# Memory rows in two parts, another order of block 1's tail units, and a cap on filling work

## The chip, the core and the metric

The kernel runs on one core of a Trainium2 chip. Its engines work side by side, each through its own instructions in order: TensorE (PE in the profile, PEld for its weight loads), VectorE (DVE), ScalarE (ACT), GpSimd (POOL) and SyncE (SP), which here only issues DMAs. They wait for each other through semaphores. Matmuls write PSUM; DVE and ACT read it. The metric is the device time of one execution in microseconds (us), as the median of some runs. The profile is of one execution.

## The reference

A sequence of 2048 rows of width 640 goes through an attention with a recurrent memory, in segments of 32 rows, and then through a feed-forward part. In short (layer norms and residual sums around it):

```python
for s in range(64):
    h = concat([mem, x[32*s:32*s+32]])         # 8 memory rows + 32 rows
    q, k, v = h @ Wq, h @ Wk, h @ Wv           # 32 heads of 128
    scores = q @ k.T * scale                   # masked: memory sees all,
    p = softmax(where(mask, scores, -1e9))     # rows see memory and their past
    o = (p @ v) @ Wo                           # 40 x 640
    mem = o[:8]                                # needed by the next segment
    outs.append(o[8:])
h = x + concat(outs)
out = h + relu(layernorm(h) @ w1 + b1)**2 @ w2 + b2
```

The memory rows make the 64 segments a chain: segment s+1 can't project its memory rows before segment s has its output.

## The kernel before

**Steps and blocks.** A step is a segment; four steps are a block of 128 rows. Of a segment, `step` (L445) handles the 8 memory rows and the first 24 rows together as 32 rows of `hT`. The last 8 rows, the tail, are projected for a whole block at once (32 rows): `tail_units` (L316) for their q, k and v, and `wo_tail_units` (L355) for their output. Tail work doesn't belong to the chain of memory rows. It is cut into units of four to eight matmuls, kept in the list `fill`, and PE gets some of them wherever a step would leave it waiting.

**A step, on PE, in order.** Projections for q, k, q, k (two halves each, L466), 20 matmuls each; memory scores of the first half (`sm`); values `v`; scores of the second half; token scores; one or two filling units; memory values (`values`, L516); two units; 64 matmuls of the output projection of the memory rows and of the segment before (`pw`, L652); two units; token values of the step before (`token_values`, L408); all units left; then the next step's q projection into the tile `pq`.

**From pw to the next hT.** `wo_out` (L271) sums the four row groups of `pw`: ACT copies the upper two to `otmp` (L281), then the lower two (L282), DVE adds `pw` and `otmp` into `o` (L283). `mem_to_hT` (L370) turns `o` into the columns of `hT` (L374). All four work on 160 columns, which are five column chunks (DC = 5) of 32. The q projection takes its chunks one after the other: matmuls of chunk c need only chunk c of `hT`. `pw`, `pq` and `sm` are tiles of the pool `chn` with one buffer, so each of them waits until the one before has been read.

**What sets the order.** The code's order is the order on each engine. `portion(s)` (L872) takes units from `plan`, which is sorted by due step, at a pace of 8 a step; a unit that is due is taken in any case. It can take more than 8 where the pace had fallen behind. `late` holds small works for DVE (turns of tail rows among them) that run at the start of a step.

**The start.** `start` (L775) projects segment 0 while the weights come in, and between them the tail values of blocks 0 to 11, then q and k of block 1's tails, as far as PE has time; what is left goes to `fill` for step 0, which (`ready`) runs ten units ahead of its values and `SEG0[k]` units ahead of each quarter of its `pw`. The quarters need the eight pieces of `wo` in the order of their loads (L149). Tail values are cast from PSUM by ACT to a tile and written to DRAM (`vt_d`, L337), from where they are read again later. Eighteen places of tiles that are not in use yet are `parked` for this (blocks 1 to 9, two each). Without a parked place the row goes into one of four buffers of `row` (L247), which also take every q and k row on its way from PSUM (ACT, L244 and L251) to DVE's turn (L256). All these DMAs are issued by SP in the order of the code; at most eight are under way, as each waits for the landing of the eighth before it.

Of the kernel before, what the change touches and what calls it, by code (L numbers as in the profile page):

```python
# [9 lines left out]
ALU = mybir.AluOpType  # L10
# [6 lines left out]
def kernel(  # L17
# [16 lines left out]
    nc = tc.nc  # L34
# [3 lines left out]
    SEG = 32  # L38
# [4 lines left out]
    DC = D // 128  # L43
# [95 lines left out]
    for q in range(4):  # L139
        nc.vector.tensor_copy(out=o0[32 * q:32 * q + 32, :].rearrange("m (c f) -> m c f", f=32),  # L140
                              in_=mem0[:].rearrange("m (c q f) -> m q c f", q=4, f=32)[:, q])
# [80 lines left out]
    def proj(w, by, lhs, n, ps, c0, c1):  # L222

        if by == "columns":
            wr = w[:].rearrange("p (c g j n k e) -> p c n k g j e", c=DC, g=G, n=2, j=4, k=4)
        elif by == "half":
            wr = w[:].rearrange("p (c k j n e) -> p c n k j e", c=DC, k=G, n=2, j=4)
        else:
            wr = w[:].rearrange("p (c k n f) -> p c n k f", c=DC, k=G, n=2)
        for c in range(c0, c1):  # L230
            for k in range(4):
                nc.tensor.matmul(ps[32 * k:32 * k + 32, :], lhsT=lhs(c), rhs=wr[:, c, n, k], start=(c == 0), stop=(c == DC - 1))  # L232

    def mmtile():
        return mm.tile([128, 512], F32, tag="mm", name="ps")
# [32 lines left out]
                    nc.tensor.matmul(pw[32 * j:32 * j + 32, c0:c0 + DH], lhsT=lhs(p), rhs=wov2[:, head(p), ch],  # L268
                                     start=(h == 0), stop=(h == 15))

    def wo_out(pw):  # L271
        o = o_ring[0]
        o_ring.append(o_ring.pop(0))
        tmp = s2.tile([128, DQ], F32, tag="otmp", name="otmp")

        def blocks(p0, p1, c0):
            return pw[p0:p1, c0:c0 + DH].rearrange("p (c x) -> p c x", x=64)[:, :, 0:32]

        def five(x):
            return x.rearrange("p (c f) -> p c f", f=32)  # L280
        nc.scalar.copy(out=five(tmp[0:64]), in_=blocks(64, 128, 0))  # L281
        nc.scalar.copy(out=five(tmp[64:128]), in_=blocks(0, 64, 64))  # L282
        nc.vector.tensor_tensor(out=five(o[:]), in0=blocks(0, 128, 32), in1=five(tmp[:]), op=ALU.add)  # L283
        return o

    fill, late, mid, nook = [], [], [], []
# [1 line left out]
    def run(q, n, held=None, stop=False):  # L288
        while n > 0 and q:
            out = q.pop(0)()  # L290
            if out and held is not None:
                held.append(out)
                if stop:
                    break
            elif out:
                out[1]()
            n -= 1
# [15 lines left out]
    def tail_rows(b, c):  # L313
        return hTts[b // 4][:, c, b % 4].rearrange("p k s -> p (k s)")

    def tail_units(b, which):  # L316
        w = {"q": wq, "k": wk, "v": wv}[which]
        lhs = lambda c: tail_rows(b, c)
        st = {}

        def unit(n, c):
            def f():
                if c == 0:
                    st[n] = mmtile()
                proj(w, "columns" if which != "v" else "order", lhs, n, st[n], c, c + 1)
                return (True, lambda: tail_out(b, which, n, st[n][:])) if c == DC - 1 else None
            return f
        return [unit(n, c) for n in range(2) for c in range(DC)]
# [38 lines left out]
            return f  # L367
        return [unit(k) for k in range(10)]

    def mem_to_hT(o, b, sp):  # L370

        at = sp * SEG
        hc = hTs[b % 2][:].rearrange("p (c r) -> p c r", c=DC)
        nc.vector.transpose(out=hc[:, :, at:at + SEG], in_=o[:].rearrange("p (c f) -> p c f", f=32))  # L374

    def tails_in(b, sp, n=None):
        hs = slice(0, H) if n is None else slice(n * 16, n * 16 + 16)
# [67 lines left out]
    def step(b, sp, v=None):  # L445
        s = b * 4 + sp
# [3 lines left out]
        if not ready:  # L450
            v = s2.tile([128, EG], BF16, tag="v", name="v")
# [178 lines left out]
        if nook:  # L630
# [9 lines left out]
                                op=ALU.mult)  # L640
        pk = s1.tile([128, HG, 32], BF16, tag="pk", name="pk")
        nc.gpsimd.tensor_tensor(out=pk[:], in0=ek[:, :, 0:SEG], in1=rk[:].unsqueeze(2).to_broadcast([128, HG, SEG]),
                                op=ALU.mult)

        if not last:
            pw = chn.tile([128, 512], F32, tag="ch", name="pw")
            if ready:
                for k in range(4):
                    run(fill, SEG0[k])
                    wo_rounds(lambda p: oT[:, p, M:NK], pw, [2 * k + h + 4 * (k // 2) for h in (0, 1, 4, 5)])  # L650
            else:
                wo_rounds(lambda p: oT[:, p, M:NK], pw, range(16))  # L652
            o = wo_out(pw)
            mem_to_hT(o, (s + 1) // 4, (s + 1) % 4)
            if s > 1:
                store_main(o, s - 2)
            held = []
            run(fill, 2, held)
            if s:
                token_values(s - 1, *prevs[-2], po, False)  # L660
                token_out(s - 1, po)
            run(fill, 100, held)
            settle(held, True)
            for _, f in held:
                late.append((0.35, f, s + 1))
            tails_in((s + 1) // 4, (s + 1) % 4)
# [5 lines left out]
        for u in range(2):  # L672
            nc.gpsimd.tensor_tensor(out=pTx[:, u], in0=pTt[:, u, 0:TL].unsqueeze(1).to_broadcast([128, 4, TL]),
                                    in1=same[:], op=ALU.mult)
# [48 lines left out]
    parked += [(hnT0[:, c, :], True) for c in range(DC)] + [(ht0[k][:, 0:512], True) for k in range(NK4)]  # L723
    parked += [(t, True) for t, _ in halves(oTts[1][:].rearrange("p h r -> p (h r)"))]
    writes = []
    SEG0 = (0, 0, 8, 8)
    hnTs = [hnT0[:], ck(DC * NT).rearrange("p (c t) -> p c t", c=DC)]
    ots = [ck(D) for _ in range(4)]
    fxs = [ck(D) for _ in range(4)]
# [45 lines left out]
    def start():  # L775

        v = s2.tile([128, EG], BF16, tag="v", name="v")
        main = rows_of(0, 0)
        pas = [pop.tile([128, 2, 512], F32, tag="po%d" % h, name="pa%d" % h) for h in range(2)]
        banks = [pas[h][:, n, :] for h in range(2) for n in range(2)]  # L780
        banks += [mmtile()[:] for _ in range(3)] + [chn.tile([128, 512], F32, tag="ch", name="pv")[:]]
        for c in range(DC):
            for k in range(4):
                for n in range(2):
                    proj(wv, "order" if k else "half", (lambda c, b=k - 1: tail_rows(b, c)) if k else main, n,
                         banks[2 * k + n], c, c + 1)
        for n in range(2):
            evac(n == 1, v[:, n * 512:(n + 1) * 512], banks[n])
        for k in range(1, 4):
            for n in range(2):  # L790
                tail_out(k - 1, "v", n, banks[2 * k + n], n == 1)
        units = tail_units(3, "v")
        run(units, DC)
        ln_transpose(("t", 1))()
        ln_norm(("t", 2))
        run(units, DC)
        units += [u for b in range(4, 8) for u in tail_units(b, "v")]

        def stream(which, w, dst, turn=None):
            pas = [pop.tile([128, 2, 512], F32, tag="po%d" % h, name="pa%d" % h) for h in range(2)]  # L800
            for c in range(DC):
                for n in range(2):
                    proj(w, "columns", main, n, pas[0][:, n, :], c, c + 1)
                for n in range(2):
                    proj(w, "columns", lambda c: tail_rows(0, c), n, pas[1][:, n, :], c, c + 1)
                if c == 2 and turn:
                    turn()
                if c < DC - 1:
                    run(units, 7 + c % 2)
            run_late(0, 100)  # L810
            for n in range(2):
                row = rowtile()[:]
                evac_row(which, row, pas[0][:, n, :])
                tail_out(0, which, n, pas[1][:, n, :])
                flip(row, dst, n)
                run_late(0, 100)
                if which == "k":
                    tails_in(0, 0, n)

        stream("q", wq, qT, lambda: ln_transpose(("t", 2))())  # L820
        for n in range(2):
            spread(n)
        tails_v_in(0, nc.gpsimd, 0, 1)
        run(units, 10)
        parked.append((s1.tile([128, D], BF16, tag="xn", name="parkx")[:, 0:512], False))
        units += [u for b in range(8, 12) for u in tail_units(b, "v")]
        stream("k", wk, kT)
        units += tail_units(1, "q") + tail_units(1, "k")
        run(units, 10)
        fill.extend(units)  # L830
        return v
# [28 lines left out]
    for b in range(2, NB):  # L860
        for which in "qk":
            u = tail_units(b, which)
            plan += [(4 * b - 3 + (which == "k"), 4 * b - 5, u[DC * n:DC * n + DC]) for n in range(2)]
    for b in range(12, NB):
        u = tail_units(b, "v")
# [6 lines left out]
    def portion(s):  # L872
        n = round(8.0 * (s - 2)) - paced[0]
        got = []
        while True:
            if not begun:
                ready = [p for p in plan if p[1] <= s]
                if not ready:
                    break
                plan.remove(ready[0])  # L880
                begun.append(ready[0])
            d, _, u = begun[0]
            if len(got) >= n and d > s:
                break
            got.append(u.pop(0))
            if not u:
                begun.pop()
        paced[0] += len(got)
        return got
# [57 lines left out]
    for t in range(S // NT):  # L947
        hnT = hnTs[t % 2]
        more = t + 1 < S // NT
        got, hts, mvs = {}, {}, {}  # L950
        if t == 0:
            got = got1
# [3 lines left out]
        for fc in range(FC):  # L956
# [13 lines left out]
            if more and fc >= 1 and (fc - 1) // 3 < NK4:  # L970
                k, stage = divmod(fc - 1, 3)
# [30 lines left out]
        for q in range(NK4):  # L1002
            pr, hf = q // 2, q % 2
            cs = slice(hf * DH, (hf + 1) * DH)
# [4 lines left out]
            for hh in range(2):  # L1009
                k = pr + 2 * hh  # L1010
# [44 lines left out]
```

## Time and profile before

| | us |
|---|---|
| median of three runs | 981.39 (980.9 to 983.57) |
| the profiled execution: its time | 980.93 |
| its span, first to last instruction | 979.1 |
| PE busy | 939.5 |
| DVE, ACT, POOL busy | 652.7, 525.1, 282.1 |
| mean granted PE clock | 0.995 |

How it is read: in the groups, the waits and the timeline a line names an engine, a line of the kernel, an operation and the tiles that it writes and reads. In the waits, the numbers are us in total, how many times, and the longest. In the timeline, the first two numbers are the start and the length in us, and brackets hold the idle time before and what ended it. Steps 1 to 63 lie between 73 and 847 us, about 12.2 us each; the feed-forward part fills the end.

### The profile page before, as it was taken

How to read it: one execution, taken by the hardware profiler on the slowest of the kernel's cores; microseconds unless marked ns; L12 is line 12 of the kernel's file. 1: busy time of each engine (PE TensorE's matmuls, PEld its weight loads, DVE VectorE, ACT ScalarE, POOL GpSimd, SP SyncE). 2: the span in 40 equal slices, each digit the busy share in tenths (PEclk: the TensorE clock that was granted, in tenths of full speed). 3: DMA queues.
4: the chain of work that ended last, by engine and by line, in shares of the span. 5: the costliest groups of instructions: out<-in, count | busy, mean ns of one | idle time of the engine just before them, and what ended most of it. 6: DMA issues, size and time to landing. Idle time of an engine off the chain costs nothing.

```text
span 979.1 us, 55574 instructions
## 1 busy us (share of the span) xinstructions
PE 939.5 (96%) x24760; PEld 547.4 (56%) x24760; DVE 652.7 (67%) x1942; ACT 525.1 (54%) x1271; POOL 282.1 (29%) x870
## 2 busy tenths in 40 slices
PE   6948999999999999999999999999999999999998
PEld 2425555555555555555555655555555656555555
DVE  5137777777676767776767676777776787566542
ACT  2425555566556556566656565665655655523321
POOL 2112323233223232323232323232323233263210
PEclk9979999999999999999999999999999999999999
DMA  9980110101010201010101010101010211543320
GB/s 355 400 273 28 14 31 9 30 15 31 14 37 14 31 13 31 9 31 8 31 14 31 14 31 11 33 12 33 11 33 6 53 40 24 165 137 79 98 55 27
DMA packets 65871, 56.62 MB, mean 58 GB/s; under 512 B 37384, under 2 KB 61712, under 8 KB 63712
## 3 DMA queue, kind: packets, MB, share of 16 engines
q1 hardware_dynamic: 65392, 52.74, 19.3%
q8 instruction: 194, 3.18, 1.4%
q14 instruction: 45, 0.37, 0.1%
q0 software_dynamic: 224, 0.33, 0.1%
q10 hardware_dynamic: 16, 0.01, 0.0%
HBM read 38.37 MB, written 9.44 MB: 49 GB/s over the span
## 4 chain that ended last, share of the span: by engine, by line
PE 84%; DVE 6%; DMA 4%; ACT 3%; SPq 2%; issue 1%; POOL 0%; ACTq 0%; DVEq 0%
PE ps L232 26%; PE pw L268 16%; PE px L232 12%; PE pq L232 7%; PE y L1012 6%; PE ps L960 6%; PE ps L268 3%; PE po L522 2%; DMA wq<-in_A_Wq_dram 2%; PE po L415 2%; SPq L149 2%; DVE kT L476 1%; PE sm L486 1%; DMA wo<-in_A_Wo_dram 1%; PE ps L575 1%
## 5 line engine op out<-in xcount | busy, mean ns | idle before, releaser
L232 PEld LDWEIGHTS <-hT 128*32 128x32 bf16 x7680 | 193.7, 96 | 189.9 <-DVE hT L374 23.2
L268 PE MATMUL pw<-wo,oT 128*32 128x320 bf16 x4224 | 161.9, 301 | 13.1 <-DVE oT L242 11.2
L232 PE MATMUL ps<-wk,hT 128*32 128x512 bf16 x2520 | 157.8, 379 | 0.0
L268 PEld LDWEIGHTS <-oT 128*32 128x32 bf16 x4224 | 118.9, 97 | 53.1 <-DVE oT L242 28.8
L256 DVE STREAM_TRANSPOSE qT<-row 128x512 bf16<-128x512 bf16 x128 | 90.7, 709 | 58.4 <-ACT row L251 55.0
L639 POOL TENSOR_TENSOR pkt<-ek,rk 128x64 bf16<-128x64 bf16 x64 | 18.9, 296 | 284.1 <-DVE rk L637 284.1
L232 PE MATMUL ps<-wv,hT 128*32 128x512 bf16 x1260 | 89.7, 378 | 0.0
L232 PE MATMUL pq<-wq,hT 128*32 128x512 bf16 x1260 | 79.5, 381 | 8.6 <-DVE hT L374 6.3
L244 ACT CAST row<-ps 128x512 bf16<-128x512 f32 x105 | 61.7, 590 | 37.8 <-PE ps L232 37.3
L426 ACT CAST oT<-po 128x512 bf16<-128x512 f32 x128 | 68.7, 589 | 20.4 <-PE po L420 18.9
L232 PE MATMUL px<-wq,hT 128*32 128x512 bf16 x1260 | 79.0, 379 | 0.0
L232 PE MATMUL px<-wv,hT 128*32 128x512 bf16 x1260 | 79.0, 378 | 0.0
L434 POOL COPY qz<-qT 128x96 bf16<-128x96 bf16 x126 | 33.6, 267 | 154.8 <-DVE qT L256 154.8
L968 ACT ACTIVATE wv<-ps,b1f 128x512 bf16<-128x512 f32 (+1 forms) x56 | 37.6, 672 | 66.6 <-PE ps L960 65.3
L633 ACT ACTIVATE ek<-tk 128x320 bf16<-128x320 f32 x64 | 30.1, 471 | 74.9 <-DVE tk L628 66.5
L256 DVE STREAM_TRANSPOSE kT<-row 128x512 bf16<-128x512 bf16 x65 | 46.2, 711 | 32.2 <-ACT row L244 32.0
L232 PEld LDWEIGHTS <-hTt 128*32 128x32 bf16 x1920 | 46.2, 96 | 27.9 <-issue 2.3
L1012 PE MATMUL y<-wq,wk 128*128 128x320 bf16 x416 | 58.9, 299 | 0.2
L473 ACT CAST row<-ps 128x256 bf16<-128x256 f32 x126 | 40.8, 375 | 28.5 <-PE ps L232 28.5
L251 ACT ACTIVATE row<-px 128x512 bf16<-128x512 f32 x63 | 37.6, 597 | 30.2 <-PE px L232 30.2
L486 PEld LDWEIGHTS <-qz 128*32 128x32 bf16 x2016 | 34.8, 94 | 32.4 <-POOL qz L436 3.7
L251 ACT ACTIVATE row<-pq 128x512 bf16<-128x512 f32 x63 | 37.6, 597 | 25.5 <-PE pq L232 25.0
(129 smaller groups left out, 1674.7 us busy)
## 6 DMA issues: line engine op xcount, KB each, us to landing
wv<-in_A_Wv_dram SPq DMA_DIRECT2D x5, 1024.0 KB
wq<-in_A_Wq_dram SPq DMA_DIRECT2D x5, 1024.0 KB
wk<-in_A_Wk_dram SPq DMA_DIRECT2D x5, 1024.0 KB
wo<-in_A_Wo_dram SPq DMA_DIRECT2D x8, 640.0 KB
o_all<-o SPq DMA_DIRECT2D x256, 7.5 KB
vt<-vt_d SPq DMA_DIRECT2D x60, 64.0 KB
xt<-in_A_x_dram SPq DMA_DIRECT2D x19, 160.0 KB
wq<-in_B_w_dram SPq DMA_DIRECT2D x1, 2080.0 KB
```

Of the source, the lines that this page charges most:

```text
L232: nc.tensor.matmul(ps[32 * k:32 * k + 32, :], lhsT=lhs(c), rhs=wr[:, c, n, k], start=(c == 0), stop=(c == DC - 1))
L244: nc.scalar.copy(out=out_, in_=in_)
L251: nc.scalar.mul(out=row, in_=ps, mul=scale)
L256: nc.vector.transpose(out=dst[:, n * 16:(n + 1) * 16, 0:32], in_=row.rearrange("p (h e) -> p h e", e=32))
L268: nc.tensor.matmul(pw[32 * j:32 * j + 32, c0:c0 + DH], lhsT=lhs(p), rhs=wov2[:, head(p), ch], start=(h == 0), stop=(h == 15))
L426: nc.scalar.copy(out=oTg[:, gs, :, 0:SEG], in_=po[1][h][:, :, 0:256].rearrange("p g (i q) -> p g i q", q=32))
L434: nc.gpsimd.tensor_copy(out=d.rearrange("p a (j f) -> p a j f", j=3)[:, :, :, 0:M], in_=src[:, :, 0:3, :])
L473: nc.scalar.copy(out=row[:, u * 256:(u + 1) * 256], in_=ps[:, u * 256:(u + 1) * 256])
L486: nc.tensor.matmul(sm[32 * g:32 * g + 32, 0:NK], lhsT=qz[:, p, :], rhs=kT[:, p, :], start=(j == 0), stop=(j == 3), skip_group_check=True)
L960: nc.tensor.matmul(ps[:], lhsT=w1[:, c, fc * 128:(fc + 1) * 128], rhs=hnT[:, c, :], start=(c == 0), stop=(c == DC - 1))
L968: nc.scalar.activation(out=r[:, 0:w], in_=ps[:, 0:w], func=ACT.Relu, bias=b1f[:, fc:fc + 1], scale=1.0)
L1012: nc.tensor.matmul(y[hh][:, 0:DH], lhsT=f1T[:, fc, k * 128:(k + 1) * 128], rhs=w2[:, fc, cs], start=(fc == 0 and not hf), stop=(fc == FFUL ...
```

## The change

Three parts.

1. `wo_out` gets a second argument, `then`. With it, the two copies, the add and the turn into `hT` are done for column chunks 0 to 2 (96 columns) and then for chunks 3 and 4 (64 columns). `step` uses that for the memory rows; the tails' output (`wo_tail_out`) and the last step's `end_output` still use one part.
2. In `start`, the tail values of blocks 8 and 9 and block 1's tail queries come ahead of `stream("k", ...)`, then block 1's tail keys, then the tail values of blocks 10 and 11. `SEG0`, which gives the units ahead of the quarters of step 0's `pw`, is (0, 1, 8, 9) where it was (0, 0, 8, 8); as it is a maximum, all that is left is run.
3. A portion is closed at nine units, unless the next one is due.

```diff
-    def wo_out(pw):
+    def wo_out(pw, then=None):
...
-        nc.scalar.copy(out=five(tmp[0:64]), in_=blocks(64, 128, 0))
-        nc.scalar.copy(out=five(tmp[64:128]), in_=blocks(0, 64, 64))
-        nc.vector.tensor_tensor(out=five(o[:]), in0=blocks(0, 128, 32), in1=five(tmp[:]), op=ALU.add)
+        for c0, c1 in ((0, 3), (3, DC)) if then else ((0, DC),):
+            cs = slice(c0, c1)
+            nc.scalar.copy(out=five(tmp[0:64])[:, cs], in_=blocks(64, 128, 0)[:, cs])
+            nc.scalar.copy(out=five(tmp[64:128])[:, cs], in_=blocks(0, 64, 64)[:, cs])
+            nc.vector.tensor_tensor(out=five(o[:])[:, cs], in0=blocks(0, 128, 32)[:, cs], in1=five(tmp[:])[:, cs], op=ALU.add)
+            if then:
+                mem_to_hT(o, *then, cs)
         return o
...
-    def mem_to_hT(o, b, sp):
+    def mem_to_hT(o, b, sp, cs=slice(0, DC)):
...
-        nc.vector.transpose(out=hc[:, :, at:at + SEG], in_=o[:].rearrange("p (c f) -> p c f", f=32))
+        nc.vector.transpose(out=hc[:, cs, at:at + SEG], in_=o[:].rearrange("p (c f) -> p c f", f=32)[:, cs])
...
-            o = wo_out(pw)
-            mem_to_hT(o, (s + 1) // 4, (s + 1) % 4)
+            o = wo_out(pw, ((s + 1) // 4, (s + 1) % 4))
...
-    SEG0 = (0, 0, 8, 8)
+    SEG0 = (0, 1, 8, 9)
...
-        units += [u for b in range(8, 12) for u in tail_units(b, "v")]
+        units += [u for b in (8, 9) for u in tail_units(b, "v")] + tail_units(1, "q")
         stream("k", wk, kT)
-        units += tail_units(1, "q") + tail_units(1, "k")
+        units += tail_units(1, "k") + [u for b in (10, 11) for u in tail_units(b, "v")]
...
-            if len(got) >= n and d > s:
+            if len(got) >= min(n, 9) and d > s:
```

## The prediction

> **What bounds the kernel now.** I read the page's chain of waits first, then the waits, then the timeline in three places. PE carries nearly the whole chain, so only time in which PE stands still can be won, and what makes it stand longer is lost.
>
> ```profile
> PE 939.5 (96%) x24760; PEld 547.4 (56%) x24760; DVE 652.7 (67%) x1942; ACT 525.1 (54%) x1271; POOL 282.1 (29%) x870
> PE 84%; DVE 6%; DMA 4%; ACT 3%; SPq 2%; issue 1%; POOL 0%; ACTq 0%; DVEq 0%
> ```
>
> The waits name what the change touches: a long stop in step 0 and a short one at each step's end.
>
> ```profile
> PEld L268 <- DVE oT L242: 28.8, 59, 10.1
> ...
> PEld L232 <- DVE hT L374: 23.2, 55, 1.9
> ...
> ACT row L251 <- DMA vt_d<-row: 9.9, 1, 9.9
> ```
>
> **The stop in step 0**, in the chain's pieces in order of time, and in the timeline:
>
> ```profile
> 50.14 10.31 DMA wo<-in_A_Wo_dram
> ...
> 60.51 2.84 DMA vt_d<-row
> ...
> 63.43 0.60 ACT row L251
> ```
>
> ```profile
> 65.60 2.32 PE L268 MATMUL pw<-wo,oT 128*32 128x320 bf16 x32 [9.96 <-DVE oT L242]
> ...
> 73.09 1.26 PE L232 MATMUL pq<-wq,hT 128*32 128x512 bf16 x20 [1.54 <-DVE hT L374]
> ```
>
> PE is said to wait for DVE; the root is a buffer. The four `row` buffers hold the tail values of blocks 10 and 11, whose writes stand in SP's queue behind the `wo` loads. Block 1's tail queries need such a buffer, and ACT, in order, can't copy oT before the write lands at 63.35. The clock falls meanwhile, as busy times by stage show (a line ends with granted clock, DMA share, GB/s):
>
> ```profile
> 54.90:58.30 3.40, 0.74 (x48) 0.35 (x40) 0.00 (x0) 0.00 (x0) 0.00 (x0) 1.00 1.07 359
> 58.30:65.60 7.30, 0.00 (x1) 0.01 (x2) 1.54 (x4) 1.24 (x3) 0.00 (x0) 0.50 0.99 296
> 65.60:68.60 3.00, 3.00 (x44) 1.58 (x48) 1.96 (x5) 0.47 (x1) 0.25 (x1) 0.51 0.41 102
> ```
>
> **A step's end**, steps 27 to 28:
>
> ```profile
> 405.62 0.29 ACT L281 COPY otmp<-pw 64x160 f32<-64x160 f32 x1 [0.62 <-PE pw L268]
> ...
> 405.92 0.28 ACT L282 COPY otmp<-pw 64x160 f32<-64x160 f32 x1
> ...
> 406.24 0.33 DVE L283 TENSOR_TENSOR o<-pw,otmp 128x160 bf16<-128x160 f32 x1 [0.48 <-ACT otmp L282]
> ...
> 406.60 0.35 DVE L374 STREAM_TRANSPOSE hT<-o 128x160 bf16<-128x160 bf16 x1
> ...
> 407.00 1.26 PE L232 MATMUL pq<-wq,hT 128*32 128x512 bf16 x20
> ```
>
> The last pw matmul starts 0.34 before the first copy, so from it to pq are 1.72 us. PE's own work in between takes, by the boundaries that it limits, 1.92 us with 6 filling units, 2.35 with 8, 2.79 with 10: 0.66 + 0.212 per unit, thus 1.72 with the usual 5. The fill just covers the chain of copies. Seven boundaries with at most two units stand open; there PE starts pq 0.93 to 1.27 us after its matmul before:
>
> ```profile
> 97.27 1.05 PE L232 MATMUL pq<-wq,hT 128*32 128x512 bf16 x16 [1.03 <-DVE hT L374]
> ```
>
> **The change part by part.** The sum is against the profiled execution, 980.93 us (span 979.1 and 1.83 around it); it lies 0.46 under the median, 981.39.
>
> *Two parts at the step's end.* Each of 63 steps gets two ACT and two DVE instructions more. Two things in the changed program's waits decide. pq and pw share the one `ch` buffer, so pq's first weight load waits for the last reader of pw, which is now the second add, not the first turn. And ACT's third copy waits for the first add on DVE, as both touch the same `otmp`. So six instructions lie in a row: copy, copy, add (96 columns), copy, copy, add (64 columns); both turns fall off the path (the second is done 0.3 us after pq starts and wanted 0.6 after). Durations of 96 and 64 columns are not in the trace. For the copies I take the line through ACT's PSUM rows (128 columns 266 ns, 256 375, 512 589: 0.84 a column), set at the 289 and 284 of 160: 235 and 230, then 208 and 203. For the adds the line from 324 at 160 to 423 at 256 (L625), 1.03 a column: 257 and 224. Between two copies lie 12 ns, ACT to DVE 32, DVE to ACT 35 (L492 to L495 where ACT has no wait ahead of it), DVE to pq 58. From the last pw matmul: 342 + 235 + 12 + 230 + 32 + 257 + 35 + 208 + 12 + 203 + 32 + 224 + 58 = 1880 ns, against 1720: 0.16 later. In the changed order 53 of the 62 boundaries after steps 1 to 62 have five units or fewer: 53 x 0.16 = 8.5 us; three with a little more (0.06 to 0.11 each) 0.2; six with six units are covered by PE's 1.93. Sum +8.6, the shift of units among boundaries included. Ends: every copy at ACT's shortest row (203, one element) and every add at 181 (L492, 40 columns) gives 1.70, -0.7 us; copies along the line from 203 at one element to 287 at 160 give 1.99, +15 us. The value stands nearest to rows of the same kind. Behind ACT's waiting third copy stand the fourth, the two oT casts (L426), a filling row and pq's row: the casts start 0.2 us later (1.58 after the last pw matmul, was 1.37), and px, which needs their PSUM, starts 1.2 us after they end; pq's row isn't ready sooner than ACT. DVE's pTt and pTk come 0.4 later and are wanted a step on. That costs nothing; without this cover it would be 0.2 a step, 13 us.
>
> [...]
>
> *Block 1's tail queries ahead of the last tail values, SEG0 (0, 1, 8, 9).* The number of units, rows, turns and writes stays; their places change. The queries' and keys' rows now find free buffers, so nothing holds ACT in step 0. The ten units before the values still end by 55.2; DVE has two key turns (0.7 each) before its oT cast, 54.4 + 1.4 + 0.3 = 56.1, and pw starts there, not at 65.60. Its 64 matmuls (4 x 0.5) and ten units (2.1) would end at 60.2, but the last `wo` piece lands at 60.45: last pw matmul 60.95, pq 62.8. Then the stall comes back: the value rows of blocks 10 and 11 are written in step 0, into the buffers that step 1's q and k rows need. Their four writes are moved behind nine issues of SP: four parked writes, the x load and four vt loads, at the intervals these had before (62.52 to 68.07): 60.51 + 4 x 0.51 + 0.53 + 4 x 0.70 = issue at 65.9. After vt loads a write landed 2.35 us after its issue (68.07 to 70.40): 68.25. Behind the waiting q row on ACT stand the rows of k and of the second halves, each on a write of its own, 0.5 apart; DVE's turns, POOL's spread and PE's scores wait for them. ACT copies q (0.6), DVE turns q (0.7), then k (0.7): scores at 70.4. Before, pq at 73.09 gave scores at 77.42. PE's own pace from 62.8 would be 67.1, so it stands 3.3 us. Won: 7.0, less 0.25 as the second half's rows come late: -6.7. Ends: landing after 1.95 to 2.84 us, -7.1 to -6.2. The clock: it fell at 58.3, 2.7 us after PE stopped, and half speed held to 68.6; a 3.1 to 3.3 us stand can do the same for up to 3.4 us, 0 to 1.7 lost; I take +0.9.
>
> [...]
>
> *Portions capped at 9.* PE's total work is unchanged; units move among steps 7 to 20 and 61, 62. None of the open boundaries gets a unit. What it gives: two units ahead of the values instead of one (steps 13, 17 to 20) save some 0.15 to 0.23 each, as the second values then follow the first after 0.015 instead of 0.16 to 0.24; step 62 gets a first unit (0.33), step 14 gains 0.05. Sum -1.35; ends -0.7 and -1.6.
>
> Sum: 980.93 + 8.6 - 6.7 + 0.9 - 1.35 = 982.4, for the median 0.46 more: 982.8.
>
> **The rivals.**
> 1. *Slower: small instructions hardly get cheaper.* Place: the six at each boundary. At 1.99 us the loss is 15: 989.2. It decides from 1.91, where 10.1 is lost. For it: ACT's one-element row takes 203. Against: its casts fall steadily down to 128 columns.
> 2. *The row wait in step 1 isn't there* (the writes land in time). Then 10.25 is won and no clock lost: 978.4. For: the DMA share falls to 0.41 from 65.6 on. Against: SP's order and the 2 us of every landing.
> 3. *The chain is shorter than before:* copies overlap. [...] The pairs of casts at L426 and L473 do overlap by 0.10; taken off both pairs here, 1.67, no loss but 0.5 won: 973.7. Against: in all 82 pairs L281, L282 the second starts 12 ns after the first ends.
>
> **How the numbers follow.** Forecast 0.62, own range 980 to 986 (0.45 of it within 0.3%, 0.17 above); rival 1 0.20; rival 2 0.08 (half of it faster, half within); rival 3 0.10, most of it faster. Hence faster 0.13, same 0.50, slower 0.37, where 0.3% (2.9 us) is about what a measurement of this kernel can tell from no change. The range leaves out rival 3 and the top of rival 1: 978 to 988.
>
> **What would show it.** Right: the first otmp copy to pq 1.54 us instead of 1.38 at boundaries with five units; four copies of about 0.2; the ACT wait for vt_d<-row moved from 63.4 to about 68, some 4 us long, on pq's row; pw from 56. Wrong: pq straight after the first turn; no DMA wait in step 1; a clock under 1.0 for more than 3.4 us after 62.

## The result, and the profile after

The changed kernel takes 983.24 us, the median of 20 runs (981.69 to 987.34), where the kernel before takes 981.15 beside it (20 runs, 979.42 to 983.57). The ratio is 1.0025, with a 95% interval of 1.0016 to 1.0035: some 2.5 us slower. The forecast was 982.8 in a range of 978 to 988, with "within 0.3%" as the likeliest outcome. The profiled execution took 985.02 us (span 983.0), 1.8 over its median.

Page of the changed kernel, busy time of the engines and the chain that ended last, by engine:

```profile
PE 945.4 (96%) x24749; PEld 545.2 (55%) x24760; DVE 671.1 (68%) x2068; ACT 543.2 (55%) x1397; POOL 280.7 (29%) x870
...
PE 83%; DVE 5%; DMA 4%; ACT 3%; SPq 2%; issue 2%; POOL 0%; ACTq 0%; DVEq 0%
```

The 126 more instructions on ACT and on DVE cost these engines 18 us each. In the chain "issue", time in which an engine waits for nothing that the profile shows, has gone from 1% to 2%; that was not expected (last section).

Waits of the changed kernel (us in total, times, longest):

```profile
PEld L232 <- DVE o L285: 34.8, 63, 2.0
...
PEld L268 <- DVE oT L242: 19.2, 58, 0.5
...
ACT row L251 <- DMA vt_d<-row: 4.4, 1, 4.4
...
PE ps L232 <- issue: 2.1, 1, 2.1
```

The q projection now waits for the add (L285), no longer for the turn, for 34.8 us instead of 23.2. The stop of 10.1 us ahead of step 0's `pw` is gone, and a stop of 2.1 us with no releaser is new. The wait of ACT for the tail values' write has moved and is 4.4 us long. Where these lie shows in the timeline of PE (start, length; in brackets the idle time before and what ended it):

```profile
56.01 0.84 PE L268 MATMUL pw<-wo,oT 128*32 128x320 bf16 x16 [0.42 <-DVE oT L242]
...
59.04 0.50 PE L232 MATMUL ps<-wv,hTt 128*32 128x512 bf16 x2 [2.10 <-issue]
...
63.77 0.92 PE L268 MATMUL pw<-wo,oT 128*32 128x320 bf16 x16
66.38 1.26 PE L232 MATMUL pq<-wq,hT 128*32 128x512 bf16 x20 [1.70 <-DVE o L285]
...
72.46 0.28 PE L490 MATMUL sm<-kT,qz 128*32 128x40 bf16 x16 [1.57 <-DVE kT L256]
```

The first scores of step 1 (`sm`) start at 72.46 instead of 77.42. The chain names the write that held them (start, length):

```profile
66.62 3.74 DMA vt_d<-row
70.39 0.04 ACTq L251
...
70.47 0.60 ACT row L251
```

Busy times by stage (after the stage and its length come PE, PEld, DVE, ACT and POOL; a line ends with granted clock, DMA share, GB/s):

```profile
56.90:59.00 2.10, 0.04 (x2) 0.00 (x0) 1.13 (x3) 0.47 (x1) 0.24 (x1) 1.00 1.07 350
59.00:62.40 3.40, 3.36 (x40) 2.20 (x43) 0.00 (x0) 0.00 (x0) 0.98 (x3) 0.53 0.90 269
...
70.80:72.40 1.60, 0.08 (x4) 0.09 (x1) 1.30 (x3) 1.60 (x5) 0.46 (x3) 1.00 0.87 248
```

Half speed now falls into step 0, from 59.19 to 62.60; while PE stands in step 1 the clock stays full.

The end of steps 27 to 28, the place shown before:

```profile
403.09 0.23 ACT L283 COPY otmp<-pw 64x96 f32<-64x96 f32 x1 [0.62 <-PE pw L268]
403.34 0.23 ACT L284 COPY otmp<-pw 64x96 f32<-64x96 f32 x1
...
403.60 0.26 DVE L285 TENSOR_TENSOR o<-pw,otmp 128x96 bf16<-128x96 f32 x1 [0.37 <-ACT otmp L284]
...
403.89 0.21 ACT L283 COPY otmp<-pw 64x64 f32<-64x64 f32 x1 [0.32 <-DVE o L285]
...
404.11 0.20 ACT L284 COPY otmp<-pw 64x64 f32<-64x64 f32 x1
...
404.35 0.23 DVE L285 TENSOR_TENSOR o<-pw,otmp 128x64 bf16<-128x64 f32 x1 [0.18 <-ACT otmp L284]
...
404.63 0.61 PE L232 MATMUL pq<-wq,hT 128*32 128x512 bf16 x8
```

Six instructions stand in one row, each after the one before, and `pq` follows the second add. From the first copy to `pq` are 1.54 us, where it was 1.38 (405.62 to 407.00). Counted from the start of the last `pw` matmul to `pq`, 44 of the 63 steps' ends take 1.87 to 1.89 us and 15 more 1.92 to 1.94.

Step by step, `pq` of step 1 starts 6.70 us earlier than before, that of step 2 4.83 earlier; then the lead shrinks by 0.16 at most steps (and by stops of PE, last section), is gone at step 46, and at the last step `pq` is 3.49 us late.

### The profile page after: what moved, and what is told of

Same layout as the page of the kernel before. It is cut to its first block, busy times and chain, and to the rows that moved or that the text cites. A ratio compares the mean times of both kernels' runs of the same rounds, so it can differ in the third digit from the quotient of the medians.

```text
span 983.0 us, 55758 instructions
## 1 busy us (share of the span) xinstructions
PE 945.4 (96%) x24749; PEld 545.2 (55%) x24760; DVE 671.1 (68%) x2068; ACT 543.2 (55%) x1397; POOL 280.7 (29%) x870
## 3 DMA queue, kind: packets, MB, share of 16 engines
q8 instruction: 194, 3.18, 1.4%
## 4 chain that ended last, share of the span: by engine, by line
PE 83%; DVE 5%; DMA 4%; ACT 3%; SPq 2%; issue 2%; POOL 0%; ACTq 0%; DVEq 0%
PE ps L232 25%; PE pw L268 15%; PE px L232 13%; PE pq L232 8%; PE y L1015 6%; PE ps L963 6%; PE ps L268 3%; PE po L526 2%; DMA wq<-in_A_Wq_dram 2%; SPq L149 2%; PE sm L490 1%; PE po L419 1%; PE ps L579 1%; DVE o L285 1%; DMA wo<-in_A_Wo_dram 1%
## 5 line engine op out<-in xcount | busy, mean ns | idle before, releaser
L232 PEld LDWEIGHTS <-hT 128*32 128x32 bf16 x7680 | 190.9, 96 | 201.8 <-DVE o L285 34.8
L283 ACT COPY otmp<-pw 64x96 f32<-64x96 f32 (+2 forms) x129 | 28.8, 223 | 63.3 <-PE pw L268 42.7
L285 DVE TENSOR_TENSOR o<-pw,otmp 128x96 bf16<-128x96 f32 (+2 forms) x129 | 31.3, 243 | 41.7 <-ACT otmp L284 40.5
```

What stands on the lines that cost most here:

```text
L285: nc.vector.tensor_tensor(out=five(o[:])[:, cs], in0=blocks(0, 128, 32)[:, cs], in1=five(tmp[:])[:, cs], op=ALU.add)
```

## The experiments

All ratios are to the kernel before, run beside on the same chip, with 95% intervals. 0.1% is about 1 us.

### One part undone, or one alone

e1 undoes the split in the changed kernel:

```diff
-            o = wo_out(pw, ((s + 1) // 4, (s + 1) % 4))
+            o = wo_out(pw)
+            mem_to_hT(o, (s + 1) // 4, (s + 1) % 4)
```

> The changed kernel with one edit: the memory rows are copied, summed and turned over all 160 columns again; the new order of the tail units and the cap stay. Theory (the six instructions in a row at a step's end cost 0.16 us at each boundary that the fill does not cover): the last pw matmul to pq is 1.72 us again, 53 x 0.16 = 8.5 us go, and the time is about 974.5, 0.993 of the kernel before. Rival (what the changed kernel lost in steps 2 to 63 is mostly PE standing with no releaser, 4 us more of it in its profile than before, and the longer chain is covered by the fill): the time stays between 980 and 983, and the holes without a releaser go or stay with no relation to the boundary.

e2 is the kernel before with the split alone (the three other edits undone):

> The kernel before with one edit: the memory rows in two parts; order and portions as before. Theory: 0.16 at some 53 boundaries, 8.5 to 9 us more than before, about 990 (1.009). Rival (holes without a releaser made the loss): 981 to 985, with 1.88 at the boundaries but steps that are no longer.

e3 is the kernel before with this alone:

```diff
-    SEG0 = (0, 0, 8, 8)
+    SEG0 = (0, 1, 8, 9)
...
-        units += [u for b in range(8, 12) for u in tail_units(b, "v")]
+        units += [u for b in (8, 9) for u in tail_units(b, "v")] + tail_units(1, "q")
         stream("k", wk, kT)
-        units += tail_units(1, "q") + tail_units(1, "k")
+        units += tail_units(1, "k") + [u for b in (10, 11) for u in tail_units(b, "v")]
```

> The kernel before with one edit: block 1's tail queries ahead of the last tail values, with SEG0 (0, 1, 8, 9). Theory (by the profile of the changed kernel: step 2's pq 4.83 us earlier, 0.43 of two longer chains taken off): 5.3 us less than before, about 976 (0.9946); ACT waits some 4 us for the write of the tail values in step 1 here too. Forecast of the prediction: 6.7 less with 0.9 lost to the clock, 975.4, the same within what can be told. Rival (the write landed late in that one execution by chance): it lands by 68.3 and the gain is 7, about 974.

e4 is the kernel before with `min(n, 9)` in `portion` alone:

> The kernel before with one edit: portions closed at nine units. Theory: 1.35 us less than before, about 979.8 (0.9986), with the second memory values straight behind the first in steps 13 and 17 to 20 and a filling unit in step 62. Rival: nothing, 981.2. If the three edits alone add up to the whole change (+8.6 - 5.3 - 1.35 = +2), they are independent.

| kernel | median us | ratio to before |
|---|---|---|
| e1, split undone | 972.96 | 0.9932 (0.9919 to 0.9946) |
| e2, split alone | 989.65 | 1.0100 (1.0086 to 1.0113) |
| e3, order alone | 972.46 | 0.9932 (0.9918 to 0.9945) |
| e4, cap alone | 978.93 | 0.9992 (0.9983 to 1.0001) |

The split costs 9.8 us alone (8.4 to 11.1), and its removal from the changed kernel gives 1.0025 - 0.9932 = 0.0093, 9.1 us. The order wins 6.7 (5.4 to 8.0), the cap 0.8 (-0.1 to 1.7). The sum of the parts, 9.8 - 6.7 - 0.8 = +2.3, is the whole change's 2.5, so nothing here shows that the parts depend on each other. In e1's trace the ends of steps are back at 1.72, those with six units at 1.92, and in e2's they are at 1.88. The rival, stops of PE with no releaser, is not what made the loss: e2's profile has 3.0 us of them after step 0 and that of the kernel before 2.8 (last section), and e2 is still slower by the whole price of the chain.

### What links the six instructions

e5 gives each part a tile of its own for the copies (the whole rows of the tails use a third, `otmpw`):

```diff
-        tmp = s2.tile([128, DQ], F32, tag="otmp", name="otmp")
...
+            tmp = (s2.tile([128, 32 * (c1 - c0)], F32, tag="otmp%d" % c0, name="otmp%d" % c0) if then else
+                   s1.tile([128, DQ], F32, tag="otmpw", name="otmpw"))
...
```

> The changed kernel with one edit: each of the two parts has its own tile for the copies (96 and 64 columns), so the third copy no longer waits for the first add. Theory (that wait is a link of the chain): the four copies follow each other, 0.34 + 0.23 + 0.23 + 0.21 + 0.20 and three gaps, and end 1.25 after the last pw matmul; the second add then stands behind the first turn on DVE, which ends at 1.42, and pq starts at 1.42 + 0.22 + 0.06 = 1.70. That is the 1.72 of whole rows: the time is as with whole rows, 0.993 of the kernel before. Rival (the chain's length comes from the number of instructions alone, not from that wait): pq stays at 1.88 and the time at 1.0025.

Measured: 983.66 us, 1.0019 (1.0010 to 1.0028), and 1.88 at the ends of steps. The theory failed. The third copy still waits for the first add (timeline of e5, in which the lines of the kernel are one further on):

```profile
390.61 0.26 DVE L286 TENSOR_TENSOR o<-pw,otmp 128x96 bf16<-128x96 f32 x1 [0.26 <-ACT otmp L285]
...
390.90 0.21 ACT L284 COPY otmp<-pw 64x64 f32<-64x64 f32 x1 [0.33 <-DVE o L286]
```

The rival, that the number of instructions alone makes the length, had the 1.88 and the time right, but it does not explain a wait. What the two still share is `pw`, which both read. e9 tests that: e5 with all copies ahead of all adds.

```diff
-        for c0, c1 in ((0, 3), (3, DC)) if then else ((0, DC),):
+        parts = ((0, 3), (3, DC)) if then else ((0, DC),)
+        tmps = {}
+        for c0, c1 in parts:
...
             nc.scalar.copy(out=five(tmp[64:128]), in_=blocks(0, 64, 64)[:, cs])
+            tmps[c0] = tmp
+        for c0, c1 in parts:
+            cs = slice(c0, c1)
-            nc.vector.tensor_tensor(out=five(o[:])[:, cs], in0=blocks(0, 128, 32)[:, cs], in1=five(tmp[:]), op=ALU.add)
+            nc.vector.tensor_tensor(out=five(o[:])[:, cs], in0=blocks(0, 128, 32)[:, cs], in1=five(tmps[c0][:]), op=ALU.add)
```

> The changed kernel with the two tiles for the copies and one edit more: all four copies are issued ahead of the first add. Two tiles alone left the third copy waiting for the first add, so its cause was not the tile of the copies. Theory (what orders ACT and DVE is the tile pw, which both read, whatever the columns): now the first add waits for the fourth copy and starts 1.28 after the last pw matmul instead of 0.85; add to 1.54, turn to 1.82, second add to 2.06, pq at 2.12, 0.24 later than in the changed kernel at some 58 boundaries, about 14 us: 1.017 of the kernel before. Rival (reads of different columns are free of each other): the first add starts at 0.85 beside the third copy, pq at 1.70, 0.993.

Measured: 988.02 us, 1.0088 (1.0073 to 1.0102). Timeline of e9 at the end of a step:

```profile
391.80 0.24 ACT L286 COPY otmp<-pw 64x96 f32<-64x96 f32 x1 [0.51 <-PE pw L268]
...
392.05 0.23 ACT L287 COPY otmp<-pw 64x96 f32<-64x96 f32 x1
...
392.29 0.21 ACT L286 COPY otmp<-pw 64x64 f32<-64x64 f32 x1
...
392.51 0.20 ACT L287 COPY otmp<-pw 64x64 f32<-64x64 f32 x1
...
392.75 0.26 DVE L291 TENSOR_TENSOR o<-pw,otmp 128x96 bf16<-128x96 f32 x1 [0.70 <-ACT otmp L287]
...
393.49 0.40 PE L232 MATMUL pq<-wq,hT 128*32 128x512 bf16 x4
```

The first add needs the first two copies alone, yet it waits for the fourth, 0.95 after the first copy instead of 0.51. So ACT and DVE take turns on `pw` in the order of the code, whichever columns they read. That it is `pw` follows because the add and the fourth copy share no other tile; parts with a `pw` of their own were not run. The time came out below the forecast (1.017) because `pq` follows at 2.03, not 2.12: the second add started 0.07 before the turn ahead of it on DVE ended, and took 0.18, and ends with six units, 1.92 before, lose less.

e6 adds to e5 a different buffer for `pq`:

```diff
-                ps = potile(1) if n else chn.tile([128, 512], F32, tag="ch", name="pq")[:]
+                ps = potile(1) if n else mmtile()
```

> The changed kernel with two edits: a tile of the copies for each part, and pq in the three PSUM buffers of the filling units instead of the one that pw holds. Theory (pq's first weight load then waits for the first turn alone, as the split needs it): pq at 1.42 + 0.06 = 1.48 at the seven boundaries with at most two units, 0.24 less than with whole rows, 1.7 us in all; at boundaries with five units PE's own work, 1.72, sets the start and nothing is won: about 0.991 of the kernel before. Rival 1 (pq takes a buffer that a filling unit still holds, and waits for ACT's cast of it): 0.995 to 1.01. Rival 2 (the shared buffer is not what held pq): as with two tiles alone, 0.993.

Measured: 987.28 us, 1.0057 (1.0044 to 1.0070). The shared buffer is what held `pq` behind the second add: at an open boundary `pq` (here named `ps`, as the buffer is) now follows the first turn, 1.14 after the first copy, before the second add:

```profile
91.64 0.23 ACT L284 COPY otmp<-pw 64x96 f32<-64x96 f32 x1 [0.54 <-PE pw L268]
...
92.44 0.28 DVE L379 STREAM_TRANSPOSE hT<-o 128x96 bf16<-128x96 bf16 x1
...
92.78 0.62 PE L232 MATMUL ps<-wq,hT 128*32 128x512 bf16 x8 [0.79 <-DVE hT L379]
...
92.90 0.23 DVE L286 TENSOR_TENSOR o<-pw,otmp 128x64 bf16<-128x64 f32 x1 [0.18 <-ACT otmp L285]
```

From the last `pw` matmul that is 1.48, as worked out; at ends with five units it is 1.71, PE's own work. But rival 1 took more than this gave: in 25 steps the k projection now waits (6.8 us in all; in none of e1) for a filling unit's buffer, whose cast on ACT stands behind the four copies and two casts of `oT`. The lines show step 41, which takes 12.5 us instead of e1's 12.1:

```profile
568.42 1.25 PE L232 MATMUL ps<-wq,hT 128*32 128x512 bf16 x20
569.93 1.26 PE L232 MATMUL ps<-wk,hT 128*32 128x512 bf16 x20 [0.26 <-ACT row L251]
```

e7 goes further the same way, with three parts:

```diff
-        for c0, c1 in ((0, 3), (3, DC)) if then else ((0, DC),):
+        for c0, c1 in ((0, 2), (2, 4), (4, DC)) if then else ((0, DC),):
```

> The changed kernel with one edit: three parts of two, two and one chunks (64, 64 and 32 columns) instead of two. Theory (every part adds two copies, an add and two hand-offs to one chain): 0.34 + 2 x 0.205 + 0.012 + 0.032 + 0.224, again 0.035 + 0.41 + 0.012 + 0.032 + 0.224, and 0.035 + 0.38 + 0.012 + 0.032 + 0.19 + 0.058 = 2.43 us from the last pw matmul to pq, 0.55 more than with two parts, at some 60 boundaries: 33 us, about 1015 (1.036). Rival (the second part's instructions are hidden somewhere, and the loss has another source): under 1000.

Measured: 1019.15 us, 1.0378 (1.0364 to 1.0393), and 2.42 from the last `pw` matmul to `pq` (worked out: 2.43). A third part costs 0.54 at a step's end and 1.0378 - 1.0025 = 0.0353, 35 us. Prices by shape, from the groups of e7 (behind the bar: busy us, mean ns of one | idle time before):

```profile
L285 DVE TENSOR_TENSOR o<-pw,otmp 128x64 bf16<-128x64 f32 x126 | 28.3, 225 | 36.0 <-ACT otmp L284 35.5 <-PE po L424 0.5
...
L283 ACT COPY otmp<-pw 64x64 f32<-64x64 f32 x126 | 26.2, 208 | 54.9 <-PE pw L268 36.3 <-DVE o L285 18.6
...
L285 DVE TENSOR_TENSOR o<-pw,otmp 128x32 bf16<-128x32 f32 x63 | 12.1, 192 | 9.9 <-ACT otmp L284 9.9
L283 ACT COPY otmp<-pw 64x32 f32<-64x32 f32 x63 | 11.5, 182 | 18.3 <-DVE o L285 18.3
```

Half the columns save 26 to 33 ns of some 210.

### What holds step 1 after the new order

e8 moves the writes of blocks 10 and above to POOL's queue, in the kernel with the new order alone. Blocks 10 and 11 are written in step 0; the edit takes along blocks 12 to 15, which are written later and which the expectation does not name:

```diff
-            eng = nc.sync if b else nc.gpsimd
+            eng = nc.sync if 0 < b < 10 else nc.gpsimd
```

> The kernel before with two edits: the new order of block 1's tail units with SEG0 (0, 1, 8, 9), and the tail values of blocks 10 and 11 are written to DRAM from POOL's DMA queue instead of SP's, where their writes stood behind nine issues until 66.6. Theory (the wait of ACT's q row in step 1 is those writes' landing): the first two land by 64, no DMA wait is left in step 1, the first scores of step 1 start 4.33 after pq, at 70.0 instead of 71.5, and 1.5 us are won over the new order alone: 0.9916 of the kernel before. PE's stop in step 0 (2.0 us ahead of the second quarter of pw, no releaser, 1.2 to 1.5 us after a piece of PE's code has landed) stays, as it has nothing to do with the writes. Rival (a write from POOL's queue takes as long as those of block 0, 6 to 7.6 us from issue to landing): the third and fourth row wait until about 70 and 71.5, and nothing is won.

Measured: 973.73 us, 0.9916 (0.9903 to 0.9930); step 1's scores start 4.33 after `pq`, ACT has no DMA wait there, and PE's stop in step 0 stays. But they start at 71.27, not at 70.0, as `pq` itself comes at 66.94 (65.66 in e3): against e3's 71.53 the place gives 0.26 in these two profiles, not 1.5. That the time came out as forecast is thus in part luck. Since e3 and e8 ran on different chips and differ by less than their intervals, both ran again on one chip, with a third kernel that has the cap as well:

> The kernel before with the new order of block 1's tail units alone, a second time, beside the next two kernels on one chip: 0.993 of the kernel before.

> The new order, with the writes of blocks 10 and 11 on POOL's queue, a second time. Theory (the wait for these writes costs what PE stands in step 1, 0.8 to 1.6 us in the profiles): 1 to 1.5 us less than the new order alone on the same chip, 0.9917 of the kernel before. Rival (what differed between two chips was the chips): no difference.

> The new order and the writes on POOL's queue, with the cap of nine units as well. By the prediction the cap gives 1.35 us: 0.9903 of the kernel before. By the cap alone (0.9992, interval to 1.0001) and by the two kernels with the new order, which ran the same with it and without: 0 to 0.5 us, as the new order alone with POOL's queue.

| kernel | median us | ratio to before |
|---|---|---|
| e10, order | 972.69 | 0.9930 (0.9917 to 0.9943) |
| e11, order, POOL's queue | 971.33 | 0.9919 (0.9904 to 0.9934) |
| e12, order, POOL's queue, cap | 968.80 | 0.9895 (0.9879 to 0.9910) |

In the timelines of e10 (first two lines) and e11 the wait of the scores goes:

```profile
64.53 1.26 PE L232 MATMUL pq<-wq,hT 128*32 128x512 bf16 x20 [1.53 <-DVE hT L378]
...
71.28 0.28 PE L490 MATMUL sm<-kT,qz 128*32 128x40 bf16 x16 [2.25 <-DVE kT L256]
```

```profile
65.91 1.26 PE L232 MATMUL pq<-wq,hT 128*32 128x512 bf16 x20 [1.53 <-DVE hT L378]
...
70.24 0.27 PE L490 MATMUL sm<-kT,qz 128*32 128x40 bf16 x16
```

By the ratios e11 lies 1.1 us under e10 and e8 1.6 under e3; each pair alone lies within its intervals, but both point the same way. In the profiles the scores come 1.04 earlier in e11 than in e10, though `pq` comes 1.38 later (in e11's profile the clock was at half speed for 3.41 us of step 0, in e10's it was not), and 0.26 earlier in e8 than in e3. A gain of about 1 us is likely, and not shown more closely. e12 is the fastest kernel here, 1.05% under the one before. For the cap the three comparisons give 0.8 (e4), 0 (e1 against e3) and 2.4 us (e12 against e11): it is worth about 1 us, and these runs tell it no more closely.

## Why the prediction was right, point by point

*The split.* Right: 8.6 worked out, 9.8 and 9.1 measured. The six durations, taken from lines through other shapes, came out to the nanosecond in the groups kept apart by shape (worked out 235, 230, 257, 208, 203, 224):

```profile
L285 DVE TENSOR_TENSOR o<-pw,otmp 128x96 bf16<-128x96 f32 x63 | 16.2, 257 | 28.9 <-ACT otmp L284 27.7 <-PE po L424 1.2
...
L283 ACT COPY otmp<-pw 64x96 f32<-64x96 f32 x63 | 14.8, 235 | 37.3 <-PE pw L268 37.3
L284 ACT COPY otmp<-pw 64x96 f32<-64x96 f32 x63 | 14.5, 230 | 0.7
L285 DVE TENSOR_TENSOR o<-pw,otmp 128x64 bf16<-128x64 f32 x63 | 14.1, 224 | 11.2 <-ACT otmp L284 11.2
...
L283 ACT COPY otmp<-pw 64x64 f32<-64x64 f32 x63 | 13.1, 208 | 20.6 <-DVE o L285 20.6
...
L284 ACT COPY otmp<-pw 64x64 f32<-64x64 f32 x63 | 12.8, 203 | 0.8
```

That `pq` waits for the second add because `pw` and `pq` share a buffer was right too (e6). One step of the argument was wrong: "ACT's third copy waits for the first add on DVE, as both touch the same `otmp`". The wait is there and the number stands, but its cause is `pw` (e5, e9). It matters for a repair: no second tile for the copies helps, and issuing the copies first makes it worse. The runs here show waits in the order of the code and never both engines on `pw` at once: in the changed kernel's profile none of the 258 copies overlaps one of the 129 adds, an add follows 32 ns after the second copy of its part, and the third copy 35 ns after the first add (medians). A `pw` in two PSUM tiles was not tried. And since five units of fill cover 1.72 anyway, even a split that worked could have won 0.24 only at the ends with fewer units: in e6 ten of the 63 take 1.47 to 1.49, and those with five units 1.71. At 32 columns the steps from 96 to 64 go on: for the first copy of a part (235, 208 ns) and the add (257, 224) they give an estimated 181 and 191 ns, and e7 has 182 and 192.

*The start.* The size was right (5.8 net worked out, 6.7 and 6.9 us measured in e3 and e10), its course only in part, and some of the agreement is luck. Right: `pw` begins at 56.01 (56.1 was worked out), and the row wait comes back in step 1, on pq's row, 4.4 us long. Three terms were mis-sized. The last `pw` matmul came at 64.39, not 60.95, since PE stood from 56.9 to 59.0 and then ran at half speed; no step of the prediction had this. The writes were issued at 66.6, not 65.9, and landed 3.74 us later, not 2.35, so that the scores came at 72.46, not 70.4: 5.0 won there instead of 7.0. And the clock term of 0.9 for step 1 was not there, as PE stood only 1.57 us in it. The first miss cost little in itself, for the landing of the writes set the end: in e10 the clock stayed full, `pq` started at 64.53, and the scores still came at 71.28. The other two misses work against each other: the late landing took 2.0 of the 7.0, and the 0.9 for the clock was not lost. At the scores of step 1, 5.0 are won in the changed kernel's profile, 5.9 in e3's and 6.1 in e10's; what lies between these and the times' 6.7 and 6.9 is within the intervals.

*The cap.* 1.35 worked out, 0.8 measured alone (-0.1 to 1.7): within what can be told. Its course shows in the traces: in e4 and in the changed kernel the second memory values start 0.14 us after the first in steps 17 to 20, where it was 0.29 to 0.36, and in step 62 0.28 or 0.29, where it was 0.59, about 1.0 in all. In step 13, which the prediction counted too, nothing was won (0.42 and 0.48, before 0.36).

*The rivals.* Rival 1 (1.99 at a step's end) and rival 3 (overlapping copies, 1.67) fell by the measured 1.88. Rival 2 (no row wait in step 1) fell too; the 2 us of a landing, named against it, are those of the tail values' writes (30 on SP's queue in the profile of before, each 1.8 us or more from issue to landing; the 256 rows of `o` written at its L399 land sooner, after 1.35 at the median). With the wait taken away, e11 and e8 won 1.1 and 1.6 us, not the 4.4 by which the rival lies under the forecast: it counted on `pq` at 62.8, and there `pq` comes at 65.91 and 66.94, behind PE's stop in step 0.

## What to carry to other kernels

Before work is cut into parts to let a consumer start early, list the links that the consumer and the parts share (here one PSUM buffer for `pw` and `pq`, and one PSUM tile that two engines read in turn), and what covers the place already: a chain that is not shorter for its first part only gets longer (here 1.88 us instead of 1.72). Small instructions keep most of their price (half the columns saved 26 to 33 ns of some 210 in e7), so a part more is a chain link more. Where a wait on a buffer is moved, follow the write that frees it through its queue; another queue can take that wait away (about 1 us here, on top of the new order; no run has the queue without the order).

## What the runs showed of the hardware that was not expected

*Stops of PE with no releaser.* In the 14 traces of this study PE stops 71 times with no wait that the profile shows, for over 0.45 us from the start of one of its records to the next (matmuls, weight loads and what its sequencer does); 67 of these lie at the same place when the records are counted, at 193 past a multiple of 256, and all end 1.2 to 1.6 us after a packet of the instruction queue has landed. The page of the changed kernel lists this queue, and the window 56.3 to 57.6 us holds the packet ahead of the stop in step 0 (packets, MB, share of 16 engines; first the page's line, then the window's):

```profile
q8 instruction: 194, 3.18, 1.4%
```

```profile
q8 instruction: 1, 0.02, 5.4%
```

3.18 MB over the 49,520 matmuls and weight loads are 64 bytes for each, 256 to a packet. So PE seems to run out of code and to wait for the next piece. That is argued from place and time alone; no experiment changed it. In step 0 the packet began to move at 56.38. The five packets before it had begun 10 to 36 records past a multiple of 256, and PE had passed these places at 53.10 to 53.75, so it came some 3 us late, with the DMA engines full (share 1.07); why stays open. The stop is at the same instruction in all kernels with the new order but there the landing of the writes set the end (above), except with the writes on POOL's queue. After step 0 these stops sum to 2.8 us in the profile of before, 6.0 in that of the changed kernel, 3.0 in e2's, 2.4 in e1's and 0.6 in e3's: they differ from execution to execution, and two single profiles can differ by some 3 us for this alone.

*The clock falls in steps of one window.* In every trace the granted clock changes on an even grid of 3.41 us; half speed lasted 3.41 or, where PE stood on, 10.24. Taking all such windows at full speed ahead of the last 8 us, it fell after each of the ten in which PE was busy for 0.14 to 1.33 us of 3.41, after none with more than 1.82, and between these after four (1.38, 1.55, 1.68, 1.82) and not after five (1.36, 1.48, 1.62, 1.75, 1.78). A window need not be idle throughout for that: 1.08 us of work in one, about a third, did not keep the clock in the changed kernel, where a stop of 2.10 us was enough to lose it. In e10 the stop of 1.79 us was not.
